# Attention and two matrix products on one core: the denominators of the third head group are summed on GpSimd before the array sees them

## The chip, the cores and the metric

The kernel runs on one core of a Trainium2 chip. A core has five engines that run side by side, each with its own queue, which it works off strictly in order: TensorE (PE, the matrix array; PEld is its weight load), VectorE (DVE), ScalarE (ACT), GpSimd (POOL) and SyncE (SP, which only issues DMAs). Engines wait for one another with semaphores. PSUM holds what the array writes; GpSimd has no hand in it in this kernel. The metric is the device time in microseconds (us), median of the runs: 429.25 us before the change.

## What is computed

The reference is an attention layer with normalised queries and keys, followed by two dense products with a leaky ReLU between them (batch 8, 12 heads, 448 positions, head size 64; 3584 rows, 768 columns, 2048 hidden columns).

```python
def rmsnorm(x, g):
    return x / np.sqrt(np.mean(x * x, axis=-1, keepdims=True) + 1e-06) * g
q_n, k_n = (rmsnorm(q, g_q), rmsnorm(k, g_k))
scores = scale * np.matmul(q_n, k_n.transpose(0, 1, 3, 2))
attn = np.exp(scores - np.max(scores, axis=-1, keepdims=True))
attn = attn / (np.sum(attn, axis=-1, keepdims=True) + 1e-09)
attn_out = np.matmul(attn, v)
...
h = x @ w_in
g = np.maximum(h, 0.0) + alpha * np.minimum(h, 0.0)
return (g @ w_out).astype(np.float32)
```

The sum over the last axis of `attn` is the denominator. It is this sum that the change moves.

## The kernel before

**Tiling.** The 12 heads of a batch are cut into three groups of four; `y` counts the groups over all batches, so `y` runs from 0 to 23, batch `y // 3`, and "the third group" is `y % 3 == 2`: 2, 5, 8, 11, 14, 17, 20, 23. The 448 keys are cut into seven tiles `j` of 64. A score tile (y, j) has the 64 keys of two heads on 128 partitions (index `g`) and, side by side, two more heads (index `par`) with 448 queries each: 128 x 896. `score` (line 316) makes one with matmuls on a quarter of the array's height and width each, `soft` (line 334) turns it into fp16 exponentials `expT[y][:, j]` on ScalarE.

**Denominators and values.** For a group the sum over keys is a sum over `j` and over 64 partitions. `den` (line 360) lets the array do both: `over_keys` (line 342) multiplies each of the seven tiles by a block of ones, and PSUM adds up. With weights 32 columns wide that is 7 x 4 x 2 = 56 matmuls (28 with 64 columns, for y below 9). The result has each denominator repeated over the head's 64 rows. `log` and `invert` (lines 367 and 372) form 1/x on ScalarE as exp(-ln x). `attv` (line 376) multiplies the same exponentials by the values, again 56 matmuls, and VectorE multiplies by the reciprocal into `xT`. For the first two groups of a batch (a pair, `ys` of length 2) there are two such value passes, `av` and `avb`; the third group is handled alone, with one.

**The dense part.** `up` (line 437) makes a 128-column slice of the hidden layer (6 matmuls), `down` (line 464) a 128 x 384 block of the output (16 matmuls). They are the array's filler between the attention bursts.

**Order.** Everything is written out by hand; nothing is reordered later. Lines 509 to 549 lay out "bursts": a burst holds two to four score tiles and possibly a denominator step (`dens`), a values step (`avs`), or both. Lines 603 to 675 spread `up` and `down` over the gaps after the bursts by estimated costs. The loop from line 742 emits all of it. A burst starts with two score tiles, then comes `den` or `attv`, then further score tiles. For batch 4 (groups 12 to 14) this reads:

```text
burst  score tiles (y.j)     step              gap after it
41     14.1 14.2 14.3        den (12, 13)      down, down
42     14.4 14.5 14.6 15.0   values (12, 13)   down
43     15.1 15.2 15.3        den (14)          down
44     15.4 15.5 15.6        values (14)       down, up
45     16.0 16.1             -                 down, up, up, up
```

The other batches differ only in the fillers.

**GpSimd's queue** holds, per group, two squares (`square`, line 141) and two normalisations (`scale`, line 173; SP's transposing DMAs in `turn_dma`, line 271, read their results), and per batch the issue of two DMAs for the values (`load_v`, line 111). `scale` waits for two short ScalarE operations (`root`, line 164); in burst 41 these stand behind the three exponentials of that burst, and they serve group 16. `reduce` (line 155) on VectorE waits for the squares; it is emitted inside a `down` ahead of the copy that frees the `down`'s PSUM bank (lines 479 to 484).

**PSUM.** Score tiles alternate between two double banks (`pss`); `dn`, `av` and every third or so `up` or `down` share the one double bank `acc` (`psa`); `avb` and the other `up` and `down` results share the two single banks `mm` (`psf`).

Of the kernel before, what the change touches and what calls it, by code (L numbers as in the profile page):

```python
# [9 lines left out]
FP32 = mybir.dt.float32  # L10
FP16 = mybir.dt.float16
AF = mybir.ActivationFunctionType
ALU = mybir.AluOpType
# [8 lines left out]
def kernel(  # L22
# [12 lines left out]
    nc = tc.nc  # L35

    B, H, S, D = q.shape
    DM = H * D
    DF = moe_w_in.shape[1]
    J = S // 64  # L40
    HH = H // 2
    G = HH // 2
# [4 lines left out]
    NG = B * G  # L47
    FB = DF // 4
    TD = min(7, NG)
    EB = 3  # L50
    EARLY = 3 * G
    assert G == 3

    cst = ctx.enter_context(tc.tile_pool(name="cst", bufs=1))
    ld = ctx.enter_context(tc.tile_pool(name="ld", bufs=2))
    att = ctx.enter_context(tc.tile_pool(name="att", bufs=2))
# [17 lines left out]
    nc.vector.memset(epsb, RMS_EPS)  # L74
    ones = cst.tile([128, 64], FP16, name="ones", tag="ones")
    nc.vector.memset(ones, 1.0)
    ident = cst.tile([128, 128], FP16, name="ident", tag="ident")
    make_identity(nc, ident)
    ident32 = cst.tile([32, 32], FP32, name="ident32", tag="ident32")
# [231 lines left out]
            qkT[y, nm] = t  # L311


    expT, rden, scs = {}, {}, {}

    def score(y, j):
        qT, kT = qkT[y, "q"], qkT[y, "k"]
# [16 lines left out]
    def soft(y, j):  # L334
# [4 lines left out]
            scale=QK_SCALE, bias=expb[:, 0:1],  # L339
        )  # L340

    def over_keys(accs, ys, weights):

        m = 64 if len(ys) == 1 and ys[0] < EARLY else 32
        if len(ys) == 2:
            heads = [(y, par, 0) for y in ys for par in range(2)]
        else:
            heads = [(ys[0], par, c) for par in range(2) for c in range(64 // m)]
        for j in range(J):
            for h, (y, par, c) in enumerate(heads):  # L350
                for g in range(2):
                    nc.tensor.matmul(  # L352
                        out=accs[g][ds(m * h, m), :S],
                        lhsT=weights(g, y, par, ts(c, m), j),
                        rhs=expT[y][ds(64 * g, 64), j, par, :],
                        start=(j == 0),
                        stop=(j == J - 1),
                    )

    def den(ys):  # L360
        dn = psa.tile([128, 2, 512], FP32, name="dn", tag="acc")
        over_keys(
            (dn[:, 0], dn[:, 1]), ys, lambda g, y, par, c, j: ones[ds(64 * g, 64), c]
        )
        rden[ys] = dn

    def log(ys):
        r = att.tile([128, 2, S], FP32, name="rden", tag="rden")
# [128 lines left out]
    def spin(count, wide=True):  # L497

        ps = psf.tile([128, 512], FP32, name="spin", tag="mm")
        for _ in range(count):  # L500
            nc.tensor.matmul(
                out=ps[:, :S], lhsT=idle32[:, :128] if wide else ident,
                rhs=idle32 if wide else idle, start=True, stop=True,
            )
# [10 lines left out]
    m = 0  # L515
    while m < NG * J or steps:
        n = len(bursts)
        while steps:
            ys, values = steps[0]
            if values:  # L520

                if n in dens and ys != (G - 1,):
                    break
                avs[n] = ys
                av_at.update((y, n) for y in ys)
            else:
                if n in avs or any(last_in.get(y, n) >= n for y in ys):
                    break
                dens[n] = ys
                den_at.update((y, n) for y in ys)  # L530
            steps.pop(0)
        both = len(avs.get(n, ())) == 2
        late = both or n in dens and n in avs or any(
            y >= G for y in dens.get(n, avs.get(n, ()))
        )
        limit = 2 + late + (both and avs[n][0] >= G)
        bursts.append([])
        while len(bursts[n]) < limit and m < NG * J:
            y, j = divmod(m, J)
            if j == 0 and y >= EB and av_at.get(y - EB, n) == n:  # L540

                if y - EB not in av_at or both and len(bursts[n]) < 3:
                    break
                split[n] = min(len(bursts[n]), 2)
            bursts[n].append((y, j))
            first_in.setdefault(y, n)
            if j == J - 1:
                last_in[y] = n
            m += 1
# [6 lines left out]
    def after(n, f, *a):  # L556
        post.setdefault(max(int(n), 0), []).append((f, a))
# [3 lines left out]
        for y in range(1, NG)  # L561
    }
    turn_at[2], turn_at[G] = 5, av_at[0]
    turn_at.update((y, den_at[y - 2]) for y in range(TD, NG) if y % G == 1)
    turns = {n: y for y, n in turn_at.items()}
    jobs = {}
    for y in range(G, NG):

        early = y < G + 2
        if early:  # L570
            n = turn_at[y - 1] + 1
        elif y == G + 2:
            n = den_at[G - 1]
        elif y == 2 * G:
            n = turn_at[y] - 4
        elif y % G == 1:
            n = den_at[y - 4] - 1
        elif y % G:
            n = den_at[y - G]
        else:  # L580
            n = av_at[y - 4]
        if y in (3 * G - 1, 3 * G):

            after(den_at[G] - (y < 3 * G), load_qk, y)
        else:
            at(n - (6 if early else 3 if y == 2 * G else 4 if y < 3 * G else 5), load_qk, y)
        for nm in "qk":
            if y != 2 * G:
                after(n - 2, square, y, nm)
            if early:  # L590
                after(n, reduce, y, nm, (0, 1) if (y, nm) == (G, "k") else None)
            else:
                jobs.setdefault(n + (y == G + 2 and nm == "k"), []).append((reduce, (y, nm)))
        if y == 3 * G:
            after(n, *jobs[n].pop()[:1], y, "k")
        roots[n + 1 + (y in (G + 2, 3 * G))] = y
# [20 lines left out]
    def cost(n):  # L617
        return (
            0.31 + 0.19 * len(bursts[n])
            + 1.35 * ((n in dens) + len(avs.get(n, ()))) + (0.9 if turns.get(n, TD) < TD else 0.0)  # L620
        )

    def wide(n):
# [4 lines left out]
    for b in range(B - 1):  # L628
        lo, hi = av_at[G * b + G - 1], av_at[G * b + 2 * G - 1]
        ups, old, new = (list(u) for u in periods[b])  # L630
        mlp = sum(u[0] for u in ups + old + new)
        stop = hi
        if b == 0:

            stop -= len(new)
        per = (mlp + sum(cost(n) for n in range(lo, stop))) / (stop - lo)
        clock = 0.0
        for n in range(lo, hi):
            clock += cost(n)
            free = True  # L640
            while ups or old or new:
                if old and (not ups or free and (
                    wide(n) or len(old) > sum(wide(c) for c in range(n, hi))
                )):
                    u = old.pop(0)
                elif ups:
                    u = ups.pop(0)
                else:
                    u = new.pop(0)
                gaps[n].append(u[1:])  # L650
                clock += u[0]
                free = False
                ahead = 0.5 * (UP if ups else DOWN)
                if not (ups or old) and n + len(new) < hi:
                    break
                if b == 0:
                    goal = 5 + round((NF - 5) * (n - lo) / (stop - 1 - lo))
                    if NF - len(ups) >= goal and n < stop - 1:
                        break
                    continue  # L660
                short = n in turns and len(gaps[n]) < 2
                if n < hi - 1 and not short and clock + ahead > per * (n - lo + 1):
                    break
# [78 lines left out]
    for n in range(NB):  # L742
# [33 lines left out]
        for t in tiles[:1] if wait else tiles[1:2] if lead else first_tiles:  # L776
# [3 lines left out]
                    scale(mid[n], nm)  # L780
                follow(mid[n], "k")
            soft(*t)
        if n in dens and not lead:
            den(dens[n])
        if n in avs and not lead:

            for half in (1, 0) if avs[n] == (0, 1) else (0,):
                attv(avs[n], half)
# [11 lines left out]
        if n in roots:  # L800
# [11 lines left out]
                    f(*a)  # L812
            if y >= TD:
                turn_dma(y)
        if n in dens and not lead:
            log(dens[n])
            if gaps[n] and gaps[n][0][0] is down:
                invert(dens[n])
            else:
                late = [(1, invert, (dens[n],))]  # L820
# [2 lines left out]
        spare_at, clock = [], 0.0  # L823
        taken = n + 1 in dens or n + 1 in avs or turns.get(n + 1, TD) < TD
        for k, (f, a) in enumerate(gaps[n]):
            free = 2.3 if n in dens else (0.1, 1.2, 0.0)[len(avs.get(n, ()))]
            since += 1
            if clock >= free and not turns.get(n, TD) < TD and (
                since > 2 and not (taken and k == len(gaps[n]) - 1) or free == 0.0 and k == 0
            ):  # L830
                spare_at.append(k)
                since = 0
            clock += DOWN if f is down else UP
# [29 lines left out]
            g(*c)  # L863
        if n in (0, 1, 4):
            spin(1)
        for f, a in jobs.pop(n, []) + post.get(n, []):
            f(*a)
    for k, (f, a) in enumerate(rest):
# [31 lines left out]
```

## Time and profile before

| | us |
|---|---|
| device time, median of 3 runs (428.74 to 429.75) | 429.25 |
| profiled execution: span from first to last instruction | 426.9 |
| PE busy | 414.8 |
| ACT busy | 276.2 |
| DVE busy | 209.4 |
| POOL busy | 172.1 |
| the two squares or two normalisations of a group on POOL, back to back | 3.3 to 3.5 |
| one `down` on the chain | 2.60 to 2.72 |
| one `up` on the chain | 1.13 to 1.25 |
| one exponential tile on ACT, mean | 1.00 |

The profiled execution has no time of its own in the records beside its span; the median of the runs is 2.35 us above that span, which is what lies around it (start, end). One batch in the steady part takes 49.1 us, from the start of a burst such as 41 to that of burst 49. "Busy" counts the time in which an engine has at least one instruction under way; matmuls overlap, so a group's busy time is less than count times mean.

### The profile page before, as it was taken

Reading aid. Unit: us, or ns where it says so; the run is one execution under the profiler, and the core shown is the slowest. Engines: PE = TensorE matmul, PEld = TensorE weight load, DVE = VectorE, ACT = ScalarE, POOL = GpSimd, SP = SyncE. Lnnn points to the kernel's source line nnn. Section 1 sums busy time; section 2 is a strip of 40 time slices with the busy share of each in tenths; the row PEclk is TensorE's granted clock in tenths of the full one; section 3 lists DMA queues with packets and bytes.
Section 4 is the critical chain, followed back from the end, with each engine's and each line's share of the span. In section 5 each row is a group of like instructions: output and inputs, shape, how many; then the busy total and the mean of one; then the engine's idle time right before and its main releaser. Section 6 shows DMA issues by size and latency. Waiting matters only on the chain.

```text
span 426.9 us, 11531 instructions
## 1 busy us (share of the span) xinstructions
PE 414.8 (97%) x4975; PEld 216.8 (51%) x4975; DVE 209.4 (49%) x318; ACT 276.2 (65%) x384; POOL 172.1 (40%) x137
## 2 busy tenths in 40 slices
PE   7889999999999999999999999999999999999995
PEld 3344454544455455544555555554555445555564
DVE  4875964556454455446255453635443453243321
ACT  5898887778875685767675685778575676133200
POOL 6789993574558019360556209370343000000000
PEclk9999999999999999999999999999999999999999
DMA  8999999999288804975377814973183201211033
GB/s 184 233 246 225 212 199 216 234 174 215 43 167 148 210 3 83 201 172 113 63 129 172 206 40 82 189 129 84 34 151 72 49 1 22 57 38 37 20 75 76
DMA packets 68532, 53.40 MB, mean 125 GB/s; under 512 B 35568, under 2 KB 68480, under 8 KB 68480
## 3 DMA queue, kind: packets, MB, share of 16 engines
q1 hardware_dynamic: 53680, 39.73, 42.5%
q0 software_dynamic: 13984, 11.81, 18.5%
q10 hardware_dynamic: 816, 1.11, 1.1%
q8 instruction: 39, 0.64, 0.6%
q14 instruction: 13, 0.11, 0.1%
HBM read 45.62 MB, written 11.01 MB: 133 GB/s over the span
## 4 chain that ended last, share of the span: by engine, by line
PE 90%; ACT 4%; POOL 2%; DVE 2%; issue 1%; ACTq 1%; POOLq 0%
PE op L472 29%; PE hT L418 22%; PE hTa L418 11%; PE sc L323 8%; PE opa L472 6%; PE dn L352 5%; PE av L352 5%; PE avb L352 2%; ACT expT L337 2%; POOL sq L152 1%; DVE osb L484 1%; ACTq L105 1%; PE tps L299 1%; PE hTb L418 1%; DVE ss L160 0%
## 5 line engine op out<-in xcount | busy, mean ns | idle before, releaser
L337 ACT ACTIVATE expT<-sc,expb 128x896 f16<-128x896 f32 x168 | 161.3, 1004 | 35.7 <-PE sc L323 34.9
L472 PE MATMUL op<-w_out_sb,gT 128*128 128x384 f16 (+1 forms) x752 | 126.3, 323 | 0.0
L176 POOL TENSOR_TENSOR qs<-nat,rr 128x896 f16<-128x896 f32 x41 | 69.2, 1710 | 138.9 <-issue 92.6
L472 PEld LDWEIGHTS <-gT 128*128 128x128 f16 x912 | 85.8, 98 | 64.6 <-issue 12.0
L418 PEld LDWEIGHTS <-w_in_sb 128*128 128x128 f16 x768 | 73.2, 98 | 72.4 <-issue 7.7
L418 PE MATMUL hT<-xT,w_in_sb 128*128 128x448 f16 x510 | 106.6, 353 | 0.0
L458 ACT ACTIVATE ah<-hT,cols 128x448 f16<-128x448 f32 x84 | 53.1, 634 | 45.0 <-PE hT L418 44.8
L152 POOL TENSOR_TENSOR sq<-nat 128x896 f32<-128x896 f32 (+1 forms) x47 | 75.0, 1618 | 7.6 <-DMA nat<-in_q_dram 7.5
L462 DVE TENSOR_TENSOR gT<-hT,ah 128x448 f16<-128x448 f32 x85 | 52.8, 623 | 47.5 <-ACT ah L458 47.3
L484 DVE COPY osb<-op 128x384 f32<-128x384 f32 (+1 forms) x47 | 25.8, 548 | 87.9 <-PE op L472 87.9
L323 PE MATMUL sc<-qT,kT 64*32 64x448 f16 (+1 forms) x1092 | 53.4, 356 | 4.5 <-ACT expT L337 2.2
L418 PE MATMUL hTa<-xT,w_in_sb 128*128 128x448 f16 x246 | 53.2, 352 | 0.0
L160 DVE TENSOR_REDUCE ss<-sq 128x14 f32<-128x896 f32 (+1 forms) x48 | 48.8, 1039 | 1.0 <-POOL sq L152 0.8
L458 ACT ACTIVATE ah<-hTa,cols 128x448 f16<-128x448 f32 x41 | 26.0, 635 | 31.3 <-PE hTa L418 31.3
L462 DVE TENSOR_TENSOR gT<-hTa,ah 128x448 f16<-128x448 f32 x41 | 25.6, 624 | 26.3 <-ACT ah L458 26.3
L323 PEld LDWEIGHTS <-kT 64*32 64x32 f16 (+1 forms) x1092 | 15.5, 93 | 35.5 <-issue 28.4
L472 PE MATMUL opa<-w_out_sb,gT 128*128 128x384 f16 x160 | 27.7, 326 | 0.0
L403 DVE TENSOR_TENSOR xT<-av,rden 128x896 f16<-128x896 f32 x16 | 17.5, 1091 | 20.1 <-PE av L352 15.6
L352 PEld LDWEIGHTS <-vt 64*32 64x32 f16 (+1 forms) x1260 | 19.0, 94 | 13.1 <-issue 2.1
L352 PE MATMUL dn<-expT,ones 64*32 64x448 f16 (+1 forms) x812 | 24.2, 350 | 0.9
L352 PE MATMUL av<-expT,vt 64*32 64x448 f16 (+1 forms) x812 | 24.1, 349 | 0.0
L369 ACT ACTIVATE rden<-dn 128x896 f32<-128x896 f32 x16 | 14.5, 908 | 7.3 <-PE dn L352 7.3
(60 smaller groups left out, 167.0 us busy)
## 6 DMA issues: line engine op xcount, KB each, us to landing
out_dram<-osb SPq DMA_DIRECT2D x109, 96.0 KB, 2.5
nat<-in_q_dram SPq DMA_DIRECT2D x46, 224.0 KB, 5.1
nat<-in_k_dram SPq DMA_DIRECT2D x46, 224.0 KB, 5.8
vt<-in_v_dram POOLq DMA_DIRECT2D x16, 336.0 KB, 7.6
w_in_sb<-in_moe_w_in_dram POOLq DMA_DIRECT2D x12, 256.0 KB, 8.4
w_out_sb<-in_moe_w_out_dram POOLq DMA_DIRECT2D x4, 768.0 KB, 10.5
nat<-in_q_dram ACTq DMA_DIRECT2D x2, 224.0 KB, 4.5
nat<-in_k_dram ACTq DMA_DIRECT2D x2, 224.0 KB, 6.2
```

What stands on the lines that cost most here:

```text
L152: nc.gpsimd.tensor_mul(out=sqf[:, c], in0=src[:, c], in1=src[:, c])
L160: nc.vector.tensor_reduce(out=o[:, c], in_=sqs[y, nm][:, c], axis=AXIS_X, op=ALU.add)
L176: eng.tensor_mul(out=t.rearrange("p j h d -> p h j d"), in0=nat[y, nm], in1=rr_t[y][:, "qk".index(nm)].unsqueeze(3).broadcast_to((128, 2, ...
L323: nc.tensor.matmul(out=sc[ds(64 * g + m * c, m), par, :S].rearrange("p (j c) -> p j c", j=J), lhsT=kT[ds(64 * par, 64), j, g, ts(c, m)], r ...
L337: nc.scalar.activation(out=expT[y][:, j], in_=scs[y, j][:, :, :S], func=AF.Exp, scale=QK_SCALE, bias=expb[:, 0:1],)
L352: nc.tensor.matmul(out=accs[g][ds(m * h, m), :S], lhsT=weights(g, y, par, ts(c, m), j), rhs=expT[y][ds(64 * g, 64), j, par, :], start=(j = ...
L403: nc.vector.tensor_mul(out=x, in0=av[:, :, :S], in1=r)
L418: nc.tensor.matmul(out=hT[:, :S], lhsT=w_in_sb[:, g * G + i, ts(ft, 128)], rhs=xT[b][:, g, i, :], start=(i == 0 and g == 0), stop=(i == G ...
L458: nc.scalar.activation(out=ah, in_=hT[:, :S], func=AF.Copy, scale=alpha_sb[:, ft : ft + 1])
L462: nc.vector.tensor_max(out=gT[:, ft, ds((b & 1) * S, S)], in0=hT[:, :S], in1=ah)
L472: nc.tensor.matmul(out=ops[c][:, :PW], lhsT=gT[:, ft, ts(t, 128)], rhs=w_out_sb[:, ft, ds(oh * OH + c * PW, PW)], start=(ft == 0), stop=(f ...
L484: nc.vector.tensor_copy(out=o[:, ts(c, PW)], in_=ops[c][:, :PW])
```

## The change

From the third group of batch 2 on (y = 8, 11, 14, 17, 20, 23; `PRE = 8`) the sum over the seven tiles is taken on GpSimd. `add_up` runs at the end of each burst for the tiles of that burst: six additions of an exponential tile into a float32 tile `rden`, and after the last one a multiplication by 1/8, a copy to fp16 (`hi`) and a subtraction that gives the fp16 remainder (`lo`). `hi` and `lo` are taken from the buffers of `qs` (4 of them), the sum from those of `rden` (2). `den_pre` then multiplies the two parts by a block of eights: 16 matmuls, `hi` first and then `lo` (8 in all for y = 8), into the two `mm` banks; VectorE copies the result over `rden`, and logarithm and reciprocal follow in place.

The denominators of these groups are taken in the burst of their values, in front of them, instead of one burst earlier. The burst ahead has one score tile less, that of the values one more (four, or none in the last one). The planner's costs and due times follow: squares of some groups are emitted one burst earlier, two fillers are put behind a burst of the new kind, and the spread of `up` and `down` shifts. For batch 4 the order becomes:

```text
burst  score tiles           step              gap after it    GpSimd, in its order
41     14.1 14.2 14.3        den (12, 13)      down, up        scale 16 (2), additions of 14.1 14.2 14.3
42     14.4 14.5 14.6 15.0   values (12, 13)   down            additions of 14.4 14.5 14.6, x 1/8, hi, lo, squares 18 (2)
43     15.1 15.2             -                 down, down      -
44     15.3 15.4 15.5 15.6   den_pre and       down, down      load_v (5), scale 17 (2)
                             values (14)
45     16.0 16.1             -                 down, up        scale 18 (2)
```

For y = 11 and 17 the gap of the third burst holds up, up, down; for y = 8 a single down. In the last batch bursts 67 and 68 hold no score tiles; in between stand up, up, up, down, and GpSimd has no `scale` ahead of the additions. In bursts 41 to 43 before, the squares of group 17 stood behind burst 41; now they stand behind burst 40.

The diff, cut to its core:

```diff
+    PRE = 3 * G - 1
...
+    eights = cst.tile([128, 64], FP16, name="eights", tag="eights")
+    nc.vector.memset(eights, 8.0)
...
+    def pre(ys):
+        return len(ys) == 1 and ys[0] >= PRE and ys[0] % G == G - 1
...
+    def add_up(y, j):
+
+        if j == 0:
+            return
+        e = expT[y]
+        if j == 1:
+            rden[y,] = att.tile([128, 2, S], FP32, name="rden", tag="rden")
+        s = rden[y,]
+        nc.gpsimd.tensor_add(out=s, in0=e[:, 0] if j == 1 else s, in1=e[:, j])
+        if j == J - 1:
+            hi, lo = (
+                ld.tile([128, 2, S], FP16, name="qs", tag="qs", bufs=4) for _ in range(2)
+            )
+            nc.gpsimd.tensor_scalar(
+                out=s, in0=s, scalar1=0.125, scalar2=None, op0=ALU.mult
+            )
+            nc.gpsimd.tensor_copy(out=hi, in_=s)
+            nc.gpsimd.tensor_sub(out=lo, in0=s, in1=hi)
+            parts[y] = (hi, lo)
...
+    def den_pre(ys):
+        y = ys[0]
+        m = 64 if y < EARLY else 32
+        accs = [psf.tile([128, 512], FP32, name="dnb", tag="mm") for _ in range(2)]
+        for n, part in enumerate(parts[y]):
+            for h in range(128 // m):
+                for g in range(2):
+                    nc.tensor.matmul(
+                        out=accs[g][ds(m * h, m), :S],
+                        lhsT=eights[ds(64 * g, 64), :m],
+                        rhs=part[ds(64 * g, 64), h * m // 64, :],
+                        start=(n == 0),
+                        stop=(n == 1),
+                    )
+        for g in range(2):
+            nc.vector.tensor_copy(out=rden[ys][:, g], in_=accs[g][:, :S])
+
+    def log_pre(ys):
+        r = rden[ys]
+        nc.scalar.activation(out=r, in_=r, func=AF.Ln)
...
-                if n in dens and ys != (G - 1,):
+                if n in dens and ys != (G - 1,) and not pre(ys):
                     break
...
-                if n in avs or any(last_in.get(y, n) >= n for y in ys):
+                if n in avs or any(last_in.get(y, n) + pre(ys) >= n for y in ys):
                     break
...
-        limit = 2 + late + (both and avs[n][0] >= G)
+        limit = 2 + late + (both and avs[n][0] >= G) + pre(dens.get(n, ()))
...
-                after(n - 2, square, y, nm)
+                after(n - 2 - (y % G == G - 1 and pre((y - G,))), square, y, nm)
...
-            + 1.35 * ((n in dens) + len(avs.get(n, ()))) + (0.9 if turns.get(n, TD) < TD else 0.0)
+            + (0 if n not in dens else 0.4 if pre(dens[n]) else 1.35)
+            + 1.35 * len(avs.get(n, ())) + (0.9 if turns.get(n, TD) < TD else 0.0)
...
-                if old and (not ups or free and (
+                two = n in dens and pre(dens[n]) and len(gaps[n]) < 2
+                if old and (not ups or (free or two) and (
...
-        if n in dens and not lead:
+        sums = n in dens and pre(dens[n])
+        if sums:
+            den_pre(dens[n])
+            attv(avs[n], 0, False, (log_pre, invert))
+        elif n in dens and not lead:
             den(dens[n])
-        if n in avs and not lead:
+        if n in avs and not lead and not sums:
...
-            free = 2.3 if n in dens else (0.1, 1.2, 0.0)[len(avs.get(n, ()))]
+            free = 2.9 if sums else 2.3 if n in dens else (0.1, 1.2, 0.0)[len(avs.get(n, ()))]
...
+        for y, j in tiles:
+            if pre((y,)):
+                add_up(y, j)
         for f, a in jobs.pop(n, []) + post.get(n, []):
             f(*a)
```

More of the change, by code (lines that the diff above doesn't have):

```diff
@@ L311, in turn @@
             qkT[y, nm] = t
-    expT, rden, scs = {}, {}, {}
+    expT, rden, scs, parts = {}, {}, {}, {}
+    def pre(ys):
+        return len(ys) == 1 and ys[0] >= PRE and ys[0] % G == G - 1
     def score(y, j):
@@ L563 @@
     turn_at[2], turn_at[G] = 5, av_at[0]
-    turn_at.update((y, den_at[y - 2]) for y in range(TD, NG) if y % G == 1)
+    turn_at.update(
+        (y, den_at[y - 2] - pre((y - 2,))) for y in range(TD, NG) if y % G == 1
+    )
     turns = {n: y for y, n in turn_at.items()}
@@ L578 @@
         elif y % G:
-            n = den_at[y - G]
+            n = den_at[y - G] - pre((y - G,))
         else:
@@ L814 @@
                 turn_dma(y)
-        if n in dens and not lead:
+        if n in dens and not lead and not sums:
             log(dens[n])
```

## The prediction, made before the changed kernel had run

> **What bounds the kernel now.** I read the busy shares first, then the chain of waits of one steady batch, then GpSimd's and ScalarE's timelines in the same stretch.
>
> ```profile
> PE 414.8 (97%) x4975; PEld 216.8 (51%) x4975; DVE 209.4 (49%) x318; ACT 276.2 (65%) x384; POOL 172.1 (40%) x137
> ```
>
> The array is busy 97% of the span; GpSimd has room on average, which says nothing yet about when it is free. The chain that ended last, from burst 41 on (start us, length us, what):
>
> ```profile
> 203.84 0.50 PE sc L323 x16
> 204.34 1.32 PE dn L352 x56
> 205.66 0.19 PE sc L323 x8
> 205.85 5.31 PE op L472 x32
> 211.16 0.50 PE sc L323 x16
> 211.66 1.32 PE av L352 x56
> 212.98 0.19 PE sc L323 x8
> 213.17 1.32 PE avb L352 x56
> 214.50 0.19 PE sc L323 x8
> 214.69 2.72 PE opa L472 x16
> 217.41 0.02 issue
> 217.43 0.57 DVE osb L484
> 218.00 0.04 issue
> 218.04 1.52 PE dn L352 x56
> 219.56 0.19 PE sc L323 x8
> 219.75 2.71 PE op L472 x16
> 222.45 0.50 PE sc L323 x16
> 222.96 1.32 PE av L352 x56
> 224.28 0.19 PE sc L323 x8
> ```
>
> It is the array's own queue, piece after piece, with one foreign step: the copy that frees the accumulator for `dn`. So a microsecond taken from the array, or put in front of it, is a microsecond of the kernel. In the timelines of GpSimd and ScalarE (start, length, instruction, idle before and its releaser) I look at what GpSimd does just where the additions are to go:
>
> ```profile
> 207.62 3.48 POOL L176 TENSOR_TENSOR qs<-nat,rr 128x896 f16<-128x896 f32 x2 [18.76 <-DMA out_dram<-osb]
> 211.07 6.59 POOL L152 TENSOR_TENSOR sq<-nat 128x896 f32<-128x896 f32 x4
> ```
>
> ```profile
> 207.26 0.23 ACT L171 ACTIVATE rr<-rr 128x28 f32<-128x28 f32 x1
> ```
>
> GpSimd stands idle until 207.62, 3.78 us after the burst began, because `scale` needs the root, which ScalarE ends at 207.49; the releaser named, a DMA, had long been done. Four squares take 6.59 us, 1.65 each.
>
> **What the change takes from the array.** Bursts 43 and 44 cost 219.75 - 217.41 = 2.34 and 224.47 - 222.45 = 2.02 us (224.47 is where the next piece of that chain starts, 224.28 + 0.19), together 4.36. After it: burst 43 with two score tiles 0.50; burst 44 with two tiles 0.50, `den_pre` 16 of the 56 matmuls, 16/56 x 1.32 = 0.38, values 1.32, two tiles 0.38, and 0.13 because the second `mm` bank is free only when the copy of the last down ends (0.57 + two issue steps of 0.02 and 0.04 after the down, against 0.50 of scores). That is 3.21; saved are 1.15 us per batch. For y = 8 the same sum from its own chain pieces (2.46 + 2.26 before; its values take 1.45) saves 1.38. In the last batch two pieces of 1.45 become 0.38 + 1.45, saving 1.07. Over y = 8, 11, 14, 17, 20, 23: 1.38 + 4 x 1.15 + 1.07 = 7.05 us, if nothing waits. Ups and downs are only moved; their number stays.
>
> **What it adds on GpSimd.** Seven operations with two operands and two with one, each behind the one before it in data. The nearest two-operand row is the square at 128x896, 1683 ns mean alone. A dependent instruction there has to start after the end of the last one, which shows in the first microseconds of GpSimd's timeline:
>
> ```profile
> 1.26 0.12 POOL masks.py:197 MEMSET ident<- 32x32 f32 x1
> 1.45 0.20 POOL masks.py:199 TENSOR_SCALAR_AFFINE_SELECT ident<-ident 32x32 f32<-32x32 f32 x1
> ```
>
> The 32x32 select starts 0.07 us after the memset it reads (1.26 + 0.12 = 1.38); the 128x128 pair above it, a memset of 0.20 at 0.74 and a select at 1.02, leaves 0.08. So a dependent addition is 1.68 + 0.08 = 1.76. One-operand operations of this size do not occur before. The two selects, 294 ns for 128 and 203 ns for 32 elements, give 0.95 ns an element and about 173 ns fixed, hence 1.02 us for 896, 1.10 with the gap. Bounds: 0.19 us, the copy of a single column in line 249, and 1.76, the price with two operands. I take 1.10, as the selects are the only GpSimd rows with one operand and two sizes. That an fp16 operand changes the rate no row shows on the input side; the normalisation, with fp16 output, costs 1710 ns against 1683, so type does little there. Bounds for the addition: 1.10, if the fp16 operand came free, and 1.91, the longest square (1828 ns) plus the gap. I take 1.76, the value of the nearest row.
>
> The chain: 1.68 + 5 x 1.76 for the additions, 2 x 1.10, 1.76 for the remainder: 14.44 us. `hi` is there 1.76 earlier.
>
> [...]
>
> **When it is due, and the wait it makes.** In GpSimd's queue the additions stand behind the two normalisations of the burst, which end at 207.62 + 3.48 = 211.10, that is 7.26 us after the burst's start S; exponentials are not late for them (ScalarE ends three of them by S + 3.2, and those of burst 42 before the fourth addition). So `lo` is ready at S + 7.26 + 14.44 = S + 21.70.
>
> The array in the new order, y = 14 and 20: burst 41 takes 2.01, down and up 2.66 + 1.14, burst 42 3.53 (214.69 - 211.16), a down 2.72, scores 0.50, two downs 5.35, scores 0.50, bank 0.13: S + 18.54, and without a wait `den_pre` would end at S + 18.92. With `lo` at S + 21.70, 0.05 to wake and 0.19 for its half, it ends at S + 21.94: 3.0 us of waiting. Queued behind on the array are the values, two scores and all fillers; ScalarE's logarithm, VectorE's copies and `xT` hang on it too, and they shift along with the array.
>
> For y = 11 and 17 the third gap holds up, up, down (4.99), the array arrives 0.36 earlier, and the normalisation starts at S + 3.96 there (158.66 after 154.70), so `lo` comes 0.18 later: 3.6 us. For y = 8 the third gap is a single down: by its own pieces (2.27, 3.85, 3.90, 2.72, 0.50, 2.71, 0.50, 0.13) it would end `den_pre` at S + 16.96, and `lo` comes at S + 21.92 (normalisations end at S + 7.48): 5.2 us. For y = 23 there is no normalisation ahead, and three ups and a down lie between bursts 66 and 68: no wait.
>
> Sum of waits 5.2 + 2 x 3.6 + 2 x 3.0 = 18.4; less 7.05 saved: +11.3 us. Span 426.9 + 11.3 = 438.2; with the 2.35 around it 440.5, which is the median 429.25 + 11.3.
>
> **Costed at nothing, and the cover.** The two VectorE copies (0.62 each, by the same-sized evictions in line 462), logarithm and reciprocal (0.91 + 0.95) and `xT` (1.09) lie 4.2 us behind `den_pre`; the values (1.32) and two downs (5.4) cover them, and only the `acc` bank waits for `xT`. The squares of group 18 behind `lo` end at S + 25.0, ahead of the end of `xT` at about S + 26.3, where VectorE reaches their reductions; the copy of the first down then ends near S + 29.0, its bank is wanted at S + 29.6. That cover is thin: half a microsecond each is 2.5 us in all if it is gone. The issue of `load_v` and the transposing DMAs (median 3.0 us to landing) of group 17 come 4 to 5 us later, with scores of 17 starting only three bursts on. ScalarE does as many logarithms as before, and is 65% busy. The earlier squares of 17 fill idle time ahead of 207.62. The taken buffers of `qs` and `rden` were last read a batch part earlier.
>
> **Rivals.** First, *the additions are quicker and the parts arrive in time*: speaks for it that no row has fp16 operands, against it that output type made no difference. Each microsecond off the chain is worth 5 us, for the first 3; the kernel becomes faster once the chain is under 14.44 - (18.4 - 7.05)/5 = 12.2 us, an addition of 1.45. At its lower bound, 1.10, the chain is 9.9 us, only y = 8 waits 0.7, and the time is 429.25 - 7.05 + 0.7 = 422.9. Second, *GpSimd is slower still*: one-operand steps at 1.76 make the chain 15.84, the time 447.5; with 1.91 throughout 17.2 and 454. For it: conversions, and perhaps something shared with VectorE (the pair of normalisations beside VectorE's `kT` took 3.48 instead of 3.33). Third, *the middle*: the chain between 12.2 and 13.3 (no gaps, 1.65 each, one-operand 0.85), the time 429 to 435.
>
> **How the numbers follow.** The forecast of 440.5, own range 435 to 444, has 0.58. Quicker additions with a gain have 0.14, the middle 0.07, the slower GpSimd 0.21. The range from 431 to 449 leaves out the gain and the upper part of the slower case, about 0.2. A measurement tells about 0.2%, 0.9 us, from no change; the cases together: faster 0.15, same 0.03, slower 0.82.
>
> **What would show it.** In the chain of waits the first matmuls of `dnb` wait for GpSimd's subtraction, some 3 us in each of four batches and 5 at the first; GpSimd's rows show additions near 1.7 and one-operand rows near 1.0 us; batches last about 51 us. It is wrong if the additions run under 1.45 us, if the array reaches `den_pre` later than S + 20 for some other reason, or if no wait stands in front of `dnb`.

## The result: 469.16 us, and the profile after

| | before | after |
|---|---|---|
| device time, median | 429.0 (428.56 to 429.75, 4 runs) | 469.16 (468.97 to 469.43, 4 runs) |
| ratio, 95% interval | | 1.093 (1.0914 to 1.0945) |
| span of the profiled execution | 426.9 | 467.1 |

The kernel became 9.3% slower, 40.2 us. The forecast of 440.5 had the sign and the place right and less than a third of the size; 469.16 lies far outside its range of 431 to 449. First the granted clock before the change, from its page: 40 slices of the span, each digit the clock granted to the array in tenths (9 is 90% or more).

```profile
PEclk9999999999999999999999999999999999999999
```

Then the page of the changed kernel, the engines' busy shares and the same clock:

```profile
PE 422.6 (90%) x4755; PEld 217.1 (46%) x4755; DVE 219.8 (47%) x331; ACT 275.9 (59%) x384; POOL 271.9 (58%) x191
...
PEclk9899999999959999799997999979997999999999
```

The array has 220 matmuls less and is busy 8 us longer. Behind the start-up, five slices have a clock below 9 (5, 7, 7, 7, 7), one in each batch from 2 to 6. Its waits show in the timeline of PE around burst 44 (start, length, instruction, idle before and releaser):

```profile
240.48 0.57 PE L329 MATMUL sc<-qT,kT 64*32 64x448 f16 x16
245.37 0.57 PE L400 MATMUL dnb<-qs,eights 64*32 64x448 f16 x8 [4.32 <-POOL qs L364]
247.33 0.57 PE L400 MATMUL dnb<-qs,eights 64*32 64x448 f16 x8 [1.39 <-POOL qs L365]
247.66 2.86 PE L378 MATMUL av<-expT,vt 64*32 64x448 f16 x56
```

The scores are done at 241.05; `hi` comes 4.32 us later, `lo` another 1.96. Then the values take 2.86 us. Before the change the same 56 matmuls took 1.51 in this view:

```profile
222.77 1.51 PE L352 MATMUL av<-expT,vt 64*32 64x448 f16 x56
```

GpSimd's timeline gives the chain:

```profile
226.61 3.48 POOL L179 TENSOR_TENSOR qs<-nat,rr 128x896 f16<-128x896 f32 x2 [8.06 <-ACT rr L174]
230.06 1.88 POOL L356 TENSOR_TENSOR rden<-expT 128x896 f32<-128x896 f16 x1
232.02 9.77 POOL L356 TENSOR_TENSOR rden<-rden,expT 128x896 f32<-128x896 f32 x5
241.88 2.44 POOL L361 TENSOR_SCALAR rden<-rden 128x896 f32<-128x896 f32 x1
244.38 0.93 POOL L364 CAST qs<-rden 128x896 f16<-128x896 f32 x1
245.40 1.88 POOL L365 TENSOR_TENSOR qs<-rden,qs 128x896 f16<-128x896 f32 x1
```

From 230.06 to 247.28 it is 17.2 us, with no gap above 0.1 us, where 14.44 was assumed: an addition costs 1.89, and the scaling, which has one operand, is the dearest of all. The chain of waits says the same; in the changed kernel it leaves the array and runs through GpSimd once per batch:

```profile
239.87 1.91 POOL rden L356
...
241.88 2.44 POOL rden L361
...
245.40 1.89 POOL qs L365
247.29 0.04 issue
247.33 0.57 PE dnb L400 x8
247.91 2.61 PE av L378 x44
250.52 0.49 PE sc L329 x13
251.01 5.31 PE op L519 x32
```

And the clock, by stretches of the same batch (us, then busy time and instructions of PE, PEld, DVE, ACT, POOL, the granted clock, DMA share, GB/s):

```profile
236.00:240.00 4.00, 4.00 (x27) 2.45 (x25) 3.34 (x4) 1.03 (x2) 3.84 (x3) 1.00 0.52 133
240.00:246.00 6.00, 1.63 (x28) 0.45 (x26) 0.60 (x2) 1.90 (x2) 5.76 (x4) 0.82 0.61 162
246.00:250.00 4.00, 2.67 (x64) 1.39 (x71) 1.16 (x2) 0.72 (x1) 4.00 (x3) 0.50 0.00 0
250.00:252.00 2.00, 2.00 (x39) 0.96 (x24) 0.75 (x1) 1.97 (x3) 1.89 (x3) 0.85 0.07 11
252.00:256.00 4.00, 4.00 (x27) 2.37 (x25) 2.79 (x4) 1.44 (x4) 2.45 (x2) 1.00 1.14 170
```

The clock is 1.00 up to the wait, 0.50 behind it, and then full again. A mean of 0.82 over 6 us puts its fall near 243.8, some 2.8 us after the last score; 0.85 over 2 us puts its return near 250.6, some 3.3 us after the second part's matmuls began. The forecast has no term for this.

### The profile page after: what moved, and what is told of

Its sections match the earlier page's. It is cut to its first block, busy times and chain, and to the rows that moved or that the text cites. A ratio compares the mean times of both kernels' runs of the same rounds, so it can differ in the third digit from the quotient of the medians.

```text
span 467.1 us, 11167 instructions
## 1 busy us (share of the span) xinstructions
PE 422.6 (90%) x4755; PEld 217.1 (46%) x4755; DVE 219.8 (47%) x331; ACT 275.9 (59%) x384; POOL 271.9 (58%) x191
## 4 chain that ended last, share of the span: by engine, by line
PE 62%; POOL 22%; issue 9%; ACT 4%; DVE 2%; DMA 1%; POOLq 0%; ACTq 0%
PE op L519 20%; PE hT L465 17%; POOL rden L356 12%; PE hTa L465 7%; PE sc L329 6%; PE av L378 4%; POOL qs L179 4%; PE opa L519 3%; POOL rden L361 3%; ACT expT L343 2%; POOL qs L365 2%; PE dn L378 1%; DMA nat<-in_q_dram 1%; POOL qs L364 1%; PE spin L548 1%
## 5 line engine op out<-in xcount | busy, mean ns | idle before, releaser
L519 PEld LDWEIGHTS <-gT 128*128 128x128 f16 x912 | 86.5, 98 | 67.1 <-issue 14.7
L465 PE MATMUL hT<-xT,w_in_sb 128*128 128x448 f16 x552 | 114.8, 353 | 2.0 <-DVE gT L509 2.0
L505 ACT ACTIVATE ah<-hT,cols 128x448 f16<-128x448 f32 x91 | 57.5, 633 | 47.0 <-PE hT L465 45.8
L509 DVE TENSOR_TENSOR gT<-hT,ah 128x448 f16<-128x448 f32 x92 | 57.1, 623 | 54.5 <-ACT ah L505 54.4
L356 POOL TENSOR_TENSOR rden<-rden,expT 128x896 f32<-128x896 f32 x30 | 56.7, 1891 | 2.4
L465 PE MATMUL hTa<-xT,w_in_sb 128*128 128x448 f16 x204 | 44.1, 352 | 0.0
L400 PE MATMUL dnb<-qs,eights 64*32 64x448 f16 (+1 forms) x88 | 6.7, 498 | 31.0 <-POOL qs L364 23.5
L505 ACT ACTIVATE ah<-hTa,cols 128x448 f16<-128x448 f32 x34 | 21.5, 634 | 21.3 <-PE hTa L465 21.3
L509 DVE TENSOR_TENSOR gT<-hTa,ah 128x448 f16<-128x448 f32 x34 | 21.2, 623 | 20.4 <-ACT ah L505 20.4
L378 PE MATMUL av<-expT,vt 64*32 64x448 f16 (+1 forms) x812 | 30.7, 418 | 0.0
L378 PEld LDWEIGHTS <-vt 64*32 64x32 f16 (+1 forms) x1260 | 21.7, 103 | 15.0 <-issue 5.8
L412 ACT ACTIVATE rden<-rden 128x896 f32<-128x896 f32 x6 | 5.7, 950 | 38.8 <-DVE rden L408 38.8
```

The source lines that it names most:

```text
L356: nc.gpsimd.tensor_add(out=s, in0=e[:, 0] if j == 1 else s, in1=e[:, j])
L378: nc.tensor.matmul(out=accs[g][ds(m * h, m), :S], lhsT=weights(g, y, par, ts(c, m), j), rhs=expT[y][ds(64 * g, 64), j, par, :], start=(j = ...
L465: nc.tensor.matmul(out=hT[:, :S], lhsT=w_in_sb[:, g * G + i, ts(ft, 128)], rhs=xT[b][:, g, i, :], start=(i == 0 and g == 0), stop=(i == G ...
L505: nc.scalar.activation(out=ah, in_=hT[:, :S], func=AF.Copy, scale=alpha_sb[:, ft : ft + 1])
L509: nc.vector.tensor_max(out=gT[:, ft, ds((b & 1) * S, S)], in0=hT[:, :S], in1=ah)
L519: nc.tensor.matmul(out=ops[c][:, :PW], lhsT=gT[:, ft, ts(t, 128)], rhs=w_out_sb[:, ft, ds(oh * OH + c * PW, PW)], start=(ft == 0), stop=(f ...
```

## The experiments

Theory: three things add up, namely a longer chain on GpSimd, the array's clock lost in the wait, and an array side that saves less than counted. The rivals are that GpSimd's work or the new order of the fillers costs by itself. "Before" is the kernel before, run on the same chip with each set (medians 428.8 to 429.3).

**The wait without its idle time.** Filler matmuls ahead of the denominators, into banks that these then overwrite:

```diff
+        for f in range(0 if y == NG - 1 else 32 if y == PRE else 20):
+            nc.tensor.matmul(
+                out=accs[f % 2][:, :S], lhsT=w_in_sb[:, f % KM, :128],
+                rhs=w_in_sb[:, f % KM, :S], start=True, stop=True,
+            )
         for n, part in enumerate(parts[y]):
```

> The changed kernel with filler matmuls of loaded weights (20, for y = 8 32, none for y = 23) ahead of the denominators' matmuls, into the banks that these then overwrite: the array works through most of the wait instead of standing idle. Theory A: in the changed kernel's trace the array's clock is granted at 0.5 after an idle stretch of 4.3 to 6.4 us, and the matmuls of the values, of two score tiles and part of a down run at half speed; this is worth about 10.6 us. Then the clock stays at 1.0, the values take 1.3 us again, and the time is about 458 to 460. Rival B: the slow stretch has another cause (GpSimd or the DMAs disturb the array's operands): the values stay at 2.6 us and the time at 469. Rival C: the filler itself is late and delays the denominators: above 469.

Measured: 460.41 (459.67 to 461.5), ratio 1.0738 (1.0717 to 1.076). Its PE timeline at the same place:

```profile
236.13 3.97 PE L398 MATMUL dnb<-w_in_sb 128*128 128x448 f16 x20
240.52 0.38 PE L405 MATMUL dnb<-qs,eights 64*32 64x448 f16 x8 [0.42 <-POOL qs L364]
242.49 0.38 PE L405 MATMUL dnb<-qs,eights 64*32 64x448 f16 x8 [1.58 <-POOL qs L365]
242.68 1.52 PE L378 MATMUL av<-expT,vt 64*32 64x448 f16 x56
```

The parts come no earlier, relative to the burst, yet the values are back at 1.52 us. Giving the array 112 more matmuls (32 in the first of five batches, 20 in each of the others) wins 8.8 us: theory A.

**The array's side alone.** No additions, scaling or split on GpSimd; the denominators' matmuls take two exponential tiles, so the denominators are wrong and only the array's side is left:

```diff
+        parts[y] = expT[y][:, 1], expT[y][:, 2]
...
-        for y, j in tiles:
-            if pre((y,)):
-                add_up(y, j)
```

> The changed kernel without any of GpSimd's additions, scaling and split: the denominators' matmuls take two exponential tiles instead of the two parts, so the denominators are wrong and only the array's side of the change is left. Theory A: the whole loss is the wait for GpSimd and what follows from it, so this gives the saving that was predicted for the array, 7.05 us, less about 2.5 us for banks that the new spread of fillers runs short of: 424 to 425. Rival B: the new order itself costs (banks, four score tiles in one burst, logarithm and copies behind the denominators): 429 or more.

Measured: 426.35 (425.93 to 426.86), ratio 0.9937 (0.9921 to 0.9952). So the new order itself is a gain, but of 2.5 us, between the two theories and nearer A. Its waits of the array behind VectorE, in its PE timeline:

```profile
153.00 1.29 PE L467 MATMUL hT<-xT,w_in_sb 128*128 128x448 f16 x6 [1.02 <-DVE gT L511]
169.51 2.76 PE L521 MATMUL op<-w_out_sb,gT 128*128 128x384 f16 x16 [0.25 <-DVE gT L511]
...
366.45 0.57 PE L402 MATMUL dnb<-expT,eights 64*32 64x448 f16 x15 [0.36 <-DVE osb L533]
```

The first two occur twice each: 2.9 us with the third. Three ups in a row share two banks there, since the new spread puts the one in `acc` earlier; a down follows at once on the up that feeds it. On this kernel's chain the denominators' matmuls take 0.71 to 0.72 us until the values begin, where 0.51 (0.13 + 0.38) was counted: another 1 us over five batches.

**GpSimd's side alone.** The kernel before, with `add_up` as in the change and no reader:

```diff
+        for y, j in tiles:
+            if y >= 8 and y % G == G - 1:
+                add_up(y, j)
```

> The kernel before with GpSimd's nine operations per third group added in the same places of its queue, and nobody reading their result. Theory A: GpSimd's work costs only because the array waits for its end; unread, it fills idle time, the normalisations and the loads behind them come some us later but in time: 429 to 430. Rival B: the work itself delays normalisations, transposes and loads, or disturbs VectorE and the array: 432 or more.

Measured: 495.94 (493.94 to 497.05), ratio 1.1553 (1.1521 to 1.1585), and not for either reason. In its waits the logarithm stands behind GpSimd:

```profile
ACT rden L389 <- POOL qs L359: 66.6, 6, 12.7
...
PE av L372 <- ACT rden L389: 52.2, 6, 11.6
```

The sum took a buffer of `rden`, and the same group's logarithm got that buffer next. This says nothing of GpSimd's work, so it was run again with the sum in a buffer of the squares:

```diff
-            sums[y] = att.tile([128, 2, S], FP32, name="rden", tag="rden")
+            sums[y] = ld.tile([128, 2 * J, D], FP32, name="sq", tag="sq", bufs=4).rearrange(
+                "p (h j) d -> p h (j d)", h=2
+            )
```

> The last but one run again, with the sum in a buffer of the squares (4 of them) instead of the two that logarithm and reciprocal use: there the logarithm of the same group had to wait for GpSimd's last operation, because it takes over that buffer. The result is still read by nobody. Theory A: GpSimd's work costs nothing if nobody waits for it or for its buffers: 429 to 430. Rival B: its occupancy delays normalisations, transposes and loads, or two engines' work interferes: 432 or more.

Measured: 459.67 (459.12 to 460.81), ratio 1.0716 (1.07 to 1.0733): rival B. A line of VectorE's timeline and one of PE's show how it comes about:

```profile
193.91 1.09 DVE L160 TENSOR_REDUCE ss<-sq 128x14 f32<-128x896 f32 x1 [7.48 <-POOL sq L152]
```

```profile
197.16 2.40 PE L440 MATMUL hT<-xT,w_in_sb 128*128 128x448 f16 x6 [5.07 <-DVE osb L506]
```

The squares of group 18 stand behind the sum in GpSimd's queue; their reduction on VectorE waits 7.48 us for them, the copy of a down queues behind the reduction, and the array has no bank for the next up. It waits 4.9 to 6.7 us in each of four batches, 21.7 in all, and comes back at half clock (2.40 us for six matmuls that take 1.30 at the full one). In this trace the array is busy 18.4 us at half clock in these batches; half of that, an estimated 9.2, and the 21.7 are 30.9 of the 32.0 us by which this execution (460.81) is longer than before. So the chain's length hurts even where nobody reads its result. The changed kernel's array has no such wait: there VectorE holds it up only for the 1.02, 0.25 and 0.36 us that the array-only run has too. That it is covered by the wait for `lo` is argued, not tested by itself.

**What an operation costs.** Twenty separate operations behind the last normalisation, on tiles of their own, in two passes:

```diff
+        P.tensor_mul(out=o32, in0=x32, in1=y32)
+        P.tensor_add(out=o32, in0=x32, in1=y32)
+        P.tensor_add(out=o32, in0=x32, in1=y16)
+        P.tensor_mul(out=o32, in0=x32, in1=y16)
+        P.tensor_add(out=o32, in0=x16, in1=y16)
...
+        P.tensor_scalar(out=o16, in0=x16, scalar1=0.125, scalar2=None, op0=ALU.mult)
+        P.tensor_copy(out=o32, in_=x32)
+        P.tensor_copy(out=o16, in_=x32)
```

> The kernel before with twenty separate GpSimd operations of 128x896 added behind its last normalisation, where GpSimd is idle; only their durations are read. The changed kernel's additions of float32 and fp16 took 1.89 us, its scaling by a constant 2.44 and its cast 0.94, against 1.68 for a float32 product. Theory A (the fp16 operand makes an addition dearer): float32 with float32 adds at 1.68, with fp16 at 1.89. Rival B (adding is dearer than multiplying): both additions 1.89, and the product with an fp16 operand 1.68. For the scaling: A, an arithmetic operation with a constant is slow whatever the types, 2.4; B, only with float32 output, and 1.0 with fp16 output. Time as before, 429.

Time 428.58 (one run). GpSimd's timeline of the second pass, in the order of the code:

```profile
349.71 2.08 POOL L883 TENSOR_TENSOR sq<-sq 128x896 f32<-128x896 f32 x1
351.86 2.09 POOL L884 TENSOR_TENSOR sq<-sq 128x896 f32<-128x896 f32 x1
354.03 1.89 POOL L885 TENSOR_TENSOR sq<-sq,qs 128x896 f32<-128x896 f32 x1
355.99 1.91 POOL L886 TENSOR_TENSOR sq<-sq,qs 128x896 f32<-128x896 f32 x1
357.98 1.89 POOL L887 TENSOR_TENSOR sq<-qs 128x896 f32<-128x896 f16 x1
...
364.09 2.45 POOL L890 TENSOR_SCALAR qs<-qs 128x896 f16<-128x896 f16 x1
367.36 0.94 POOL L892 CAST qs<-sq 128x896 f16<-128x896 f32 x1
```

For two operands neither theory holds. Product and sum of two float32 tiles cost the same, 2.08, and an fp16 operand makes them cheaper, 1.89. The square was no measure: it reads one tile twice, for 1.68. Nor is the number of sources alone what counts: the normalisation has two, the second a tile of only 14 numbers per partition, and takes 1.71. What sets the price among these rows no run separates. The scaling is theory A's: 2.45, also with fp16 on both sides, while cast and copy cost 0.93.

**A shorter chain.** Without the scaling:

```diff
-            nc.gpsimd.tensor_scalar(
-                out=s, in0=s, scalar1=0.125, scalar2=None, op0=ALU.mult
-            )
...
-                        lhsT=eights[ds(64 * g, 64), :m],
+                        lhsT=ones[ds(64 * g, 64), :m],
```

> The changed kernel without the scaling by 1/8 (the array multiplies by ones in place of eights): GpSimd's chain loses one operation of 2.44 us and its gap, 17.26 - 2.53 = 14.7 us, about the 14.44 that the prediction assumed. The array's wait falls by 2.53 in each of five batches: 469.2 - 12.7 = 456.5. Theory A (the array's clock halves only after an idle stretch of some length): the first idle stretch shrinks from 4.3 to 1.8 us (y = 8: 6.4 to 3.9), the clock stays at 1.0 in at least four batches, and what the filler run won, 8.8 us, comes on top: 447 to 450. Rival B (any wait at that place halves the clock): 456 to 457.

Measured: 453.64, but spread from 451.34 to 456.98 (4 runs), ratio 1.0586 (1.0533 to 1.0639): neither. In its profiled execution, of 451.4 us, the wait is 1.7 to 1.8 us for `hi` and 1.58 for `lo` in four batches, and what follows differs:

```profile
184.00 2.86 PE L375 MATMUL av<-expT,vt 64*32 64x448 f16 x56
...
237.12 1.52 PE L375 MATMUL av<-expT,vt 64*32 64x448 f16 x56
...
290.36 2.78 PE L375 MATMUL av<-expT,vt 64*32 64x448 f16 x56
...
343.21 1.98 PE L375 MATMUL av<-expT,vt 64*32 64x448 f16 x56
```

Waits of nearly equal length lose the clock in some batches and not in others; the two that lose it at once, at y = 11 and 17, are even the shorter ones (1.70 and 1.69 for `hi`, against 1.78 at y = 14 and 20).

The trace shows where they differ. In the changed kernel's trace the granted clock changes only at edges that lie whole multiples of 3.41 us apart: the half-clock stretches that end before the kernel does are 3.41, 6.83 (four of them) and 10.24 us long. With the trace of the run without the scaling cut at such edges, y = 11, 14 and 20 read as follows (columns as above, the array's busy time second, the granted clock behind POOL's):

```profile
180.29:183.70 3.41, 0.41 (x16) 0.14 (x16) 0.00 (x0) 1.51 (x2) 3.26 (x4) 1.00 0.38 86
183.70:187.12 3.42, 3.42 (x80) 1.63 (x79) 1.16 (x2) 1.47 (x2) 3.42 (x3) 0.50 0.03 7
231.49:234.90 3.41, 1.70 (x24) 0.72 (x22) 1.25 (x2) 1.83 (x2) 3.27 (x3) 1.00 1.06 259
234.90:238.31 3.41, 1.76 (x72) 1.09 (x79) 0.87 (x2) 0.08 (x1) 3.33 (x3) 1.00 0.34 109
...
340.71:344.13 3.42, 1.49 (x56) 0.90 (x63) 0.60 (x2) 0.36 (x1) 3.34 (x4) 1.00 0.22 51
344.13:347.54 3.41, 3.41 (x53) 1.48 (x31) 1.35 (x3) 2.73 (x4) 0.14 (x1) 0.50 0.99 138
```

A stretch with the array busy 0.41 or 1.49 us (12% and 44%) is followed by one at half clock; stretches with 1.70 and 1.76 (50% and 52%) are not. At y = 14 an edge splits the wait into two stretches that are each busy enough; at y = 11 almost all of it falls into one. In the first filler run a stretch busy 48% still lost the clock (y = 8) and one busy 47% kept it (y = 17), so these readings fix no limit. Edges that fall elsewhere in each execution would also give the spread of the runs; with one execution traced that is argued.

With fillers in the first part of the wait (8, and 18 for y = 8):

```diff
+        for f in range(0 if y == NG - 1 else 18 if y == PRE else 8):
```

> The run without the scaling, with filler matmuls in the first part of the wait (8, for y = 8 18, none for y = 23). Without them its values ran at half speed behind some waits (1.7 + 1.6 us of idle, y = 11 and 17) and at full speed behind others of the same length (y = 14), and its time moved between 451 and 457. Theory A (the clock drops when too much of a stretch of a few us is idle, and lengths near the limit fall on either side): with the first idle part filled all values take 1.3 us, the time is steady within 1 us, and it lies 5 x 2.53 below the first filler run, at 447.8 +- 1. Rival B (the spread has another cause, not the idle time): it still moves by several us.

Measured: 445.27 (444.78 to 446.69), ratio 1.0385 (1.0359 to 1.0411), all values at 1.52, mean clock 1.00. The spread is down from 5.6 to 1.9 us, as theory A has it, if not to 1; the time is 2.5 us below its number. In the first filler run the values of y = 8 still took 1.96, and its trace has 3.41 us at half clock there with the array busy throughout: an estimated 1.7 us. The rest of the 2.5 us is not settled.

**A version that beats both.** Five additions, the last into fp16; the array adds tile 6 itself:

```diff
+        if j < J - 2:
+            nc.gpsimd.tensor_add(out=s, in0=e[:, 0] if j == 1 else s, in1=e[:, j])
+        elif j == J - 2:
+            hi = ld.tile([128, 2, S], FP16, name="qs", tag="qs", bufs=4)
+            nc.gpsimd.tensor_add(out=hi, in0=s, in1=e[:, j])
+            parts[y] = (hi, e[:, J - 1])
```

> The changed kernel with a shorter chain on GpSimd: five additions for tiles 0 to 5, the last of which writes fp16, no scaling, no split; the array takes the sum and, as its second part, tile 6 itself, with ones. The chain is 1.89 + 4 x 1.97 = 9.8 us and ends at about S + 17.3, ahead of the array's arrival at S + 18.1 to S + 18.5, and 0.9 us after it for y = 8. Theory A (the loss is the wait for the chain and the clock that it costs): the array-only time plus 0.9, 427 to 428, faster than before by 1 to 2 us. Rival B (GpSimd's occupancy costs by itself): 430 or more.

Measured: 426.5 (426.49 to 427.82), ratio 0.9953 (0.994 to 0.9967). The only wait for GpSimd left is one of 0.81 us at y = 8. Then the same with the banks of the fillers set by hand:

```diff
+        if n + 1 in dens and pre(dens[n + 1]):
+            spare_at = [len(gaps[n]) - 1]
+            since = 0
+        elif len(gaps[n]) == 5 and all(f is up for f, _ in gaps[n]) and gaps[n][0][1][0] > 1:
+            spare_at = [2]
+            since = 2
```

> The five-tile version with the fillers' PSUM banks spread otherwise: the last filler ahead of the new denominators goes to the double bank acc, so that the denominators' two banks are free, and in gaps of five ups the third goes to acc, so that three in a row no longer share two banks. Theory A: the waits for VectorE that the array-only run showed (twice 1.02, and 0.3 to 0.4 ahead of each of the denominators) go: 423 to 425. Rival B: acc is then late for the values, and nothing is won: 427 to 428.

Measured: 422.87 (422.58 to 423.45), ratio 0.9864 (0.9851 to 0.9877), 5.9 us faster than before. From 105 to 420 us, one wait of more than 0.3 us is left on its array:

```profile
124.09 0.38 PE L395 MATMUL dnb<-qs,ones 64*64 64x448 f16 x4 [0.61 <-POOL qs L360]
```

## Why the prediction was wrong, by its own steps

| term | predicted | measured | from |
|---|---|---|---|
| array's side | -7.05 | -2.5 | array-only run: 426.35 - 428.89 |
| waits for GpSimd | +18.4 | +34.1 | first filler run less array-only run: 460.41 - 426.35 |
| clock lost in the waits | no term | +8.7 | changed kernel less first filler run: 469.16 - 460.41 |
| sum | +11.3 | +40.3 | |

The lines are differences of runs, so they add up by construction; some 1.7 us of the waits belongs to the clock, as the first filler run's trace still has 3.41 us at half clock with the array busy. Up to 1.1 us of the clock's term may come from the start-up, where the changed kernel's trace has one half-clock stretch (slice 2) and its array is at 62.29 where the filler run's is at 61.20.

**What bounds the kernel, and where the wait forms:** right. The array's queue is the bound, `den_pre` waits for `lo`, the waits stand in five batches and not in the last, and the parts of y = 23 were in time. None of the prediction's three signs of being wrong came up: the additions took 1.89, the array was ready for `den_pre` at S + 18.5, and the wait stood in front of `dnb`. They watched for a wait that is smaller or stands elsewhere, not for a dearer one.

**The size of GpSimd's chain: wrong, "I take 1.10" and "I take 1.76".** The additions took 11.73 us in place of 10.48; with the gap ahead of each, the scaling took 2.53 in place of 1.10, the cast 0.99 in place of 1.10, the remainder 1.97 in place of 1.76. Together that is 17.2, 2.8 more, in five batches 14 us of the missing 15.7. The rest is of the size of the 1.7 us at half clock that the first filler run kept, and of a later start: in burst 41 the normalisations ended 7.5 us after its first scores instead of 7.3, both in the timeline. Both prices came from the nearest row, and both rows were of another kind: a square has one source, a select is not an operation with a constant. The slower rival of 447.5 had the scaling at 1.76 as upper bound; 2.44 was outside all bounds. The slowest case, 1.91 for every step, has the measured chain of 17.2 us by luck (its scaling is too cheap, its cast too dear) and still ends at 454: it too lacks the clock and has the array's saving too large.

**The array's wait was costed as idle time only: the step that is missing.** The waits of 3.0 to 5.2 us were added up as if the array went on at its old pace. The filler run shows 8.7 us on top, with the clock at 0.50 in the records. In the changed kernel's trace the clock changes only at edges whole multiples of 3.41 us apart: it falls in or right after waits of 4.3 to 6.4 us for `hi`, at y = 14 some 2.8 us after the last score, and is back there after some 3.3 us of slow matmuls. Nor was a shorter wait safe: a stretch with the array busy 44% (run without the scaling) or 48% (first filler run) lost the clock too. So the forecast's own waits were already in danger: with a chain of about the assumed length, the run without the scaling waited 1.7 and 1.6 us around 0.4 us of work and lost the clock in three of its four equal batches.

**The array's saving: right in mechanism, too large.** Of the 4.5 us missing, 2.9 are waits for PSUM banks and inputs that the new spread of fillers makes, and about 1 the denominators' matmuls. "Ups and downs are only moved" was true and not free. The last run, with other banks and the short chain, is at 422.87, where the forecast for a chain that is in time was 422.9 including a wait at y = 8. It is another kernel, so the match is partly luck, but a saving of that size is there to be had.

With the chain at its assumed length and no clock lost, the prediction is tested directly: 445.27 - 429.27 = 16.0 us, against 11.3 plus five times 0.26 for the chain of 14.7, that is 12.6. The 3.4 between them lie within the 4.5 of the array's side.

**The cover called thin** (reductions of the squares behind `lo`) held, since everything shifted together; the second GpSimd-only run shows what it costs where the array does not wait first. Whether a later place for `den_pre` would only bring that wait forward wasn't tried.

## What to carry to other kernels

Work given to an idle engine is priced by its latency up to the point where the bound engine needs it, and every operation of that chain needs a row of the same kind: sources of the same number, size and type, and the same sort of instruction; where there is none, a few operations in idle time at the end of the kernel give it. In these runs a wait on the array cost its length and then, where it left the array busy 44% or less of one of the 3.41 us stretches (once also at 48%), its clock; so a few cheap matmuls in an unavoidable wait can win time, here 8.8 us in the first filler run. And before giving up on such a change, cut the chain to what fits: keeping five of nine operations turned +40 us into -2, and the banks of the fillers made it -6.

## What was not expected of the hardware

In the run of twenty operations a GpSimd product with a constant over 128x896 took 2.45 us with fp16 or float32, longer than the sum of two tiles (2.08 float32, 1.89 with one or two fp16 operands), and 2.6 times a cast or copy (0.93). Squaring one tile took 1.68 in the kernel before, the product of two different ones 2.08, the product with a small tile that is repeated 1.71. Dependent GpSimd operations start 0.06 to 0.1 us after the one they wait for in the changed kernel's chain, as in the first microseconds of the kernel before.

The clock of the array changes only at edges whole multiples of 3.41 us apart in the changed kernel's trace: behind the first half-clock stretch there, the stretches of one clock that end before the kernel does are 6.83 to 112.64 us long, 2 to 33 times 3.41. Of its stretches between two edges at the full clock, the seven with the array busy 42% or less (0 to 1.43 us; the last at the end of the kernel) were each followed by half clock, and all with 61% (2.08 us, y = 11) or more by the full one. In between lie readings of two other traces: in the run without the scaling 44% lost it, 50% and 52% kept it; in the first filler run 48% lost it and 47% kept it. Back from half clock more was needed: in the changed kernel a stretch with 73% busy (y = 8) was followed by another at half clock, and one with 77% (y = 20) by the full one.
